# A fused retention, gated and convolution layer stack: the last product in seven products instead of eight

## The chip, the cores and the metric

One core of a Trainium2 chip. TensorE (PE) multiplies, VectorE (DVE) and ScalarE (ACT) do the elementwise work, GpSimd (POOL) here mostly issues transfers, SyncE (SP) issues transfers only. The metric is the device time in microseconds of one execution; the median over runs is what counts. A profiled execution gives a trace of every instruction, from which all rows below are read.

## The reference

Three layers on 8 batches of 576 tokens with 512 features:

```python
# 1: retention, 8 heads of 64
ret = (q @ k.T / 8 * Dmat) @ v                 # Dmat: gamma_h ** (t - s) for s <= t
x = heads of ret side by side                  # 576 x 512
# 2: gated layer with mixing over the sequence
h = gelu(x @ w_in);  u, v = h[:, :512], h[:, 512:]
v_s = w_sg @ (layernorm(v) * g_ln) + b_sg[:, None]
x = x + (u * v_s) @ w_out
# 3: convolution gate
gate = sigmoid(sum over k < 5 of conv_w[k] * x shifted down by 4 - k)
out = (gate * (x @ w_val)) @ w_out2
```

The weights w_in, w_out, w_val, conv_w and w_out2 come as 64-bit numbers. All products need more precision than one pass of the fast matmul type gives, so each operand is held as a high and a low part (a cast on ACT, then a subtraction on DVE) and each product is three matmuls: high by high, high by low, low by high.

## The kernel before, in words

**First part (to about 394 us).** Batch by batch: retention, `x @ w_in`, the mix with `w_sg`, the gate. Places for all of it are written out by hand in `plan`, `PLACES`, `KEYS`. Beside it the weights of the later layers are fetched by SP (`fetch_second`, lines 282 and 283), decoded on ACT and DVE (`decode_second`) and stored in DRAM, two of twelve row blocks per batch (`jobs`). The four blocks of w_out are also added into the seven weight operands of a Strassen product (`sums_second`, with `SUM_AT` for the places) and stored in `w7d`; w_val and w_out2 go to `wvd` as they are. The gated activations go to DRAM (`g1d`), where POOL's accumulating transfers add up the operands t1 to t4 of the same seven products (`sum_up`).

**Second part (from about 394 us).** All operations are entered with `add(engine, us, function, reads, writes, ...)`, and `Planner.order` lays them out beforehand: each engine takes the ready operation with the longest tail, PE's order is the order of entry, and transfers land by a model of one pipe. The resulting list is fixed; on the chip every engine goes through its own in order, waiting by semaphores. With `i` the batch:
- `back(i)`: the seven products of w_out (`strassen`; 12 matmuls of 128x288 each, line 1152) from operands loaded into `raw_g` and split by `split_seven`; the sums of outputs need three snapshots of PSUM by ACT (`snap`) and three DVE additions (line 1193); the residual comes by three accumulating transfers of POOL from `x1d` (line 1204).
- `conv(i)`: for each of 4 feature blocks one ACT product (line 1226), four DVE multiply-adds (line 1232) and one sigmoid on ACT.
- `value(i)`: `plain`, four blocks of 24 matmuls (line 1252), each multiplied by the gate on DVE into `f` (line 1269).
- `final(i)`: the same `plain` with w_out2 on `f`, each output copied by ACT (line 1291) and stored.

The loop enters, for each i, back(i), conv(i), final(i-2), value(i-1); the last two rounds are final(6), value(7) and then final(7). Split operands (casts of line 158, subtractions of line 161) rotate through `NPAIR` buffers. PSUM has four buffers of two banks, taken in turn. `LATE` says in which round the operand sums of the last three batches are entered.

Of the kernel before, what the change touches and what calls it, by code (L numbers as in the profile page):

```python
# [18 lines left out]
DM = H * D  # L19
# [31 lines left out]
NPAIR, NSNAP, NOUT = 5, 3, 3  # L51
AHEAD = (B - 1, 4)
LATE = {2: (B - 3, 4), 3: (B - 2, 0), 4: (B - 1, 0)}
# [80 lines left out]
def fused_kernel(  # L134
# [31 lines left out]
    wvd = dram.tile([128, 2, 2, KT, DM], F32, name="wvd")  # L166
    w7d = dram.tile([128, 7, 2, 2, 256], F32, name="w7d")
# [17 lines left out]
    with ExitStack() as p1:  # L185
# [99 lines left out]
        def decode_second(j):  # L285
            raw = raws.pop(j)
            t = raw.rearrange("p n t -> p (n t)").rearrange("p (t n) -> p t n", t=2).bitcast(F32)
            layer, k = divmod(j, KT)
            if layer:
                return decode(t[:, 0].bitcast(F32R), t[:, 1].bitcast(F32R), raw, *small_tmp(DM)) + [  # L290
                    lambda: sync.dma_start(out=wvd[:, layer - 1, :, k], in_=t)
                ]
# [7 lines left out]
        def sums_second(k):  # L300
            x, y = pairs_of.pop(k), pairs_of.pop(k + 2)
            f, g, r = (z.bitcast(F32) for z in small_tmp(DM))
            left, right = slice(0, 256), slice(256, 512)

            def put(n, src):
                sync.dma_start(out=w7d[:, n, :, k], in_=src)
# [623 lines left out]
        def plan(kind, *args):  # L930
# [29 lines left out]
            elif kind == "v":  # L960
                now += 2.79
                at(start, v_tile, *args)
                if args[1] == 3 and i in (3, 4):
                    for j in jobs(i):
                        at(start, fetch_second, j)
# [18 lines left out]
            else:  # L984
# [15 lines left out]
        def decode_at(b, place):  # L1000
# [6 lines left out]
            for n, j in enumerate(jobs(b)):  # L1007
# [42 lines left out]
        for k in range(5):  # L1050
# [15 lines left out]
            w=[q_r.tile([128, 2, KT, DM], F32R, name="wv0")],  # L1066
# [24 lines left out]
        def split_seven(raw, key, stage=1):  # L1091

            got = {}
            for p in range(4):
                names = ORDER[2 * p : 2 * p + 2]
                src = raw[:, 2 * p : 2 * p + len(names)].rearrange("p a k n -> p (a k) n")
                k, y = split(lambda src=src: src, [(key, n) for n in names], 2 * len(names), stage)
# [13 lines left out]
        add("POOL", 0.05, lambda: pool.dma_start(out=wo, in_=w7d), (), ("wo",), 2.0, 1, 3670)  # L1111
# [13 lines left out]
        count = dict(ps=0, s=0, o=0)  # L1125
# [94 lines left out]
        def conv(i):  # L1220
            for m in range(KT):
# [7 lines left out]
                for j in range(1, TAPS):  # L1229
# [8 lines left out]
        def plain(layer, xs, put):  # L1238

            def block(o, h):  # L1240
# [3 lines left out]
                def go():  # L1244
                    ps, w = got(key), L["w"][layer]
                    for mm in range(2):
                        j = 0
                        m = slice((2 * o + mm) * 128, (2 * o + mm) * 128 + 128)
                        for k in range(KT):
                            wh, wl = w[:, 0, k, m], w[:, 1, k, m]  # L1250
# [6 lines left out]
                add("PE", 3.2, go, (("hi", at), ("lo", at), ("w", layer)), (key,), 0.24)  # L1257
                put(o, h, key)

            for h in (1, 0):  # L1260
                for o in range(2):
                    block(o, h)

        def value(i):

            def put(o, h, ps):
                add(
                    "DVE", dve_us(2 * HN),
                    lambda: dve.tensor_tensor(
                        L["f"][:, 2 * h + o], full(ps), half(L["gate"][i % 2], o, h), op=ALU.mult  # L1270
                    ), (ps, *(("gate", i % 2, 2 * o + z) for z in range(2))), (("f", o, h),),
                )

            plain(0, split_x(i), put)

        def final(i):

            def put(o, h, ps):
                to = out[:, 2 * o : 2 * o + 2, i * S + h * HN : i * S + (h + 1) * HN]
                if (o, h) == (1, 0) and i == B - 1:  # L1280
# [13 lines left out]
            xs = {  # L1294
                h: split(
                    lambda h=h: L["f"][:, 2 * h : 2 * h + 2].rearrange("p a k n -> p (a k) n"),
                    [("f", o, h) for o in range(2)], stage=2,
                ) for h in (1, 0)
            }
            plain(1, xs, put)  # L1300
# [21 lines left out]
        def load_w(n):  # L1322
            add(
                "POOL", 1.0, lambda: pool.dma_start(out=L["w"][n], in_=wvd[:, n]), (("f", 0, 1),) if n else (),
                (("w", n),), 2.0, 2 if n else 1, 2100,
            )
# [4 lines left out]
        for i in range(B + 2):  # L1331
# [22 lines left out]
    L["f"] = q_o.tile([128, 4, 2, HN], F32, name="f")  # L1354
    L["w"].append(q_o.tile([128, 2, KT, DM], F32R, name="wv1"))
    L["x2"].append(q_o.tile([128, KT, PAD + S], F32, name="x2_1"))
    L["gate"] = [q_o.tile([128, KT, S], F32, name=f"gate{n}") for n in range(2)]
    L["o"] = [q_o.tile([128, 2, HN], F32, name=f"o{n}") for n in range(NOUT)]
# [99 lines left out]
```

## Time and profile before

| | |
|---|---|
| median of 3 runs | 726.21 us (725.86 to 726.44) |
| profiled execution | 727.7 us, its span from first to last instruction 725.9 us |
| mean granted clock | 0.985 of full speed; 1.00 from 50 us on |
| busy: PE, DVE, ACT, POOL | 702.0, 521.7, 358.7, 120.8 us |
| matmuls | 8754 |

PE is the matmul row, PEld the weight loads beside it. Busy times of overlapping instructions are counted once, so a group's mean times its count can exceed its busy time. A wait is put down to the one that ended it last. Batches of the second part begin at 463.0, 499.8, 536.6, 573.4, 610.2 and 646.9 us (each with its product stretch of 84 matmuls).

### The profile page before, as it was taken

To read this page: it belongs to the slowest core of one execution; us is meant where nothing else is said; L and a number is where in the kernel's file an instruction comes from. 1 tells how busy PE (TensorE), PEld (TensorE's weight loads), DVE (VectorE), ACT (ScalarE), POOL (GpSimd) and SP (SyncE) were. 2 spreads that over 40 slices of the span, in tenths; PEclk is the share of its full clock that TensorE was granted. 3 is DMA by queue.
4 is the path that set the end of the run, shared out by engine and by line. 5 is a ranking of instruction groups with operands and counts; after the bars stand their busy time and mean duration, and the time that the engine had idled before them with its cause. 6 is when DMAs were issued, how large, how long until landed. Compare 5 with 4: busy or idle time off the path is not lost.

```text
span 725.9 us, 20052 instructions
## 1 busy us (share of the span) xinstructions
PE 702.0 (97%) x8754; PEld 672.6 (93%) x8754; DVE 521.7 (72%) x830; ACT 358.7 (49%) x651; POOL 120.8 (17%) x189
## 2 busy tenths in 40 slices
PE   3789999999999999999999999999999999999997
PEld 3689889899998998998989999999999999999997
DVE  5777788796797865957747559899795959593921
ACT  5566583653753635526436047664645444534421
POOL 0000340410501204203113022020302120202000
PEclk7799999999999999999999999999999999999999
DMA  8978439689499994696835998973847774606011
GB/s 337 326 285 288 159 107 330 196 290 345 101 266 377 257 322 163 173 372 185 219 130 116 385 309 217 282 147 115 148 164 132 212 134 160 115 18 115 34 50 65
DMA packets 63830, 147.78 MB, mean 204 GB/s; under 512 B 5376, under 2 KB 39808, under 8 KB 61952
## 3 DMA queue, kind: packets, MB, share of 16 engines
q1 hardware_dynamic: 32720, 96.33, 37.1%
q0 software_dynamic: 18992, 31.46, 22.7%
q10 hardware_dynamic: 12032, 18.73, 7.1%
q8 instruction: 68, 1.11, 0.6%
q14 instruction: 18, 0.15, 0.1%
HBM read 107.97 MB, written 52.69 MB: 221 GB/s over the span
## 4 chain that ended last, share of the span: by engine, by line
PE 89%; DMA 5%; issue 2%; DVE 2%; ACT 1%; SPq 1%; ACTq 0%
PE ps L1252 28%; PE ps_u L179 14%; PE ps_v L564 14%; PE ps_m L651 11%; PE ps L1152 11%; DMA raw_g<-g1d 4%; PE sc L420 3%; PE xo L498 3%; PE xo L490 2%; PE st L436 2%; PE ps_m L659 2%; DMA qk_sb<-in_qk 1%; DVE op L161 1%; ACT op L158 0%; SPq L375 0%
## 5 line engine op out<-in xcount | busy, mean ns | idle before, releaser
L1252 PE MATMUL ps<-op,wv 128*128 128x288 f32 x1536 | 205.1, 295 | 0.0
L1252 PEld LDWEIGHTS ps<-op,wv 128*128 128x128 f32 x1536 | 204.3, 188 | 0.0
L651 PE MATMUL ps_m<-ws,vh 128*128 128x288 f32 x768 | 113.7, 297 | 0.4 <-DVE gt L668 0.4
L1232 DVE SCALAR_TENSOR_TENSOR gate<-x,cw_sb,gate 128x576 f32<-128x576 f32 x128 | 97.2, 812 | 19.4 <-ACT gate L1226 19.4
L651 PEld LDWEIGHTS ps_m<-ws,vh 128*128 128x128 f32 x768 | 104.9, 188 | 1.5 <-DVE gt L668 0.6
L1152 PE MATMUL ps<-op,wo 128*128 128x288 f32 x672 | 91.7, 297 | 0.4 <-DVE op L161 0.4
L179 PE MATMUL ps_u<-xh,wi 128*128 128x288 f32 x448 | 91.7, 297 | 0.0
L1152 PEld LDWEIGHTS ps<-op,wo 128*128 128x128 f32 x672 | 90.6, 189 | 0.6 <-DVE op L161 0.6
L179 PEld LDWEIGHTS ps_u<-xh,wi 128*128 128x128 f32 x448 | 72.6, 188 | 0.6
L564 PE MATMUL ps_v<-wi,xh 128*128 128x512 f32 x224 | 70.8, 397 | 0.0
L179 PE MATMUL ps_u<-xl,wi 128*128 128x288 f32 x224 | 66.1, 295 | 0.0
L1204 POOL DMA_DIRECT2D x<-x1d x24 | 31.4, 1565 | 167.1 <-DVE x L1193 166.8
L510 ACT COPY xg<-xo 128x768 f32<-128x768 f32 x24 | 19.1, 797 | 73.1 <-PE xo L498 66.4
L161 DVE TENSOR_TENSOR op<-raw_g,op 128x1152 fp32r<-128x1152 f32 (+1 forms) x32 | 38.0, 1204 | 22.5 <-ACT op L158 22.5
L564 PEld LDWEIGHTS ps_v<-wi,xh 128*128 128x128 f32 x224 | 41.6, 188 | 9.6 <-ACT xh L158 0.2
L668 DVE SCALAR_TENSOR_TENSOR gt<-ps_m,g_sb,b_sb 128x288 f32<-128x288 f32 x64 | 32.8, 515 | 24.2 <-PE ps_m L659 24.1
L158 ACT CAST op<-raw_g 128x1152 fp32r<-128x1152 f32 (+1 forms) x32 | 32.6, 1036 | 35.2 <-DMA raw_g<-g1d 20.7
L581 ACT ACTIVATE vt<-ps_v 128x512 f32<-128x512 f32 x36 | 21.5, 597 | 55.6 <-PE ps_v L564 55.0
L591 POOL TENSOR_SCALAR rs<-mv 128x1 f32<-128x1 f32 x36 | 10.1, 280 | 228.3 <-DVE mv L590 216.7
L400 ACT ACTIVATE kk_sb<-kk_sb,kf_sb 128x64 f32<-128x64 f32 x184 | 47.0, 336 | 2.0 <-DMA kk_sb<-in_kk 2.0
L564 PE MATMUL ps_v<-wi,xl 128*128 128x512 f32 x112 | 44.4, 396 | 0.2 <-DVE xl L161 0.2
L637 ACT ACTIVATE u<-ps_u 128x288 f32<-128x288 f32 x64 | 26.2, 409 | 35.6 <-PE ps_u L179 35.1
(112 smaller groups left out, 1107.3 us busy)
## 6 DMA issues: line engine op xcount, KB each, us to landing
qk_sb<-in_qk SPq DMA_DIRECT2D x24, 960.0 KB, 8.3
raw_g<-g1d SPq DMA_DIRECT2D x8, 2016.0 KB, 8.5
vv_sb<-in_vv SPq DMA_DIRECT2D x24, 576.0 KB, 5.7
g1d<-g1d POOLq DMA_DIRECT2D x48, 288.0 KB, 5.0
g1d<-u SPq DMA_DIRECT2D x40, 288.0 KB, 7.7
kk_sb<-in_kk SPq DMA_DIRECT2D x24, 384.0 KB, 6.3
x1d<-xg ACTq DMA_DIRECT2D x24, 384.0 KB, 6.2
x<-x1d POOLq DMA_DIRECT2D x24, 384.0 KB, 6.5
```

Of the source, the lines that this page charges most:

```text
L158: return act.copy(dst, src) if engine is act else engine.tensor_copy(dst, src)
L161: return dve.tensor_tensor(dst, src, high.bitcast(F32), op=ALU.subtract)
L179: pe.matmul(ps[:, :n], lhs, rhs[:, k, x_cols], start=i == 0, stop=i == last)
L400: act.mul(k[:, j, n], k[:, j, n], kf_sb[:, j, n : n + 1])
L564: pe.matmul(ps, lhs, rhs, start=i == 0, stop=i == KT * 3 - 1)
L637: act.activation(bt[b]["u"][:, m, t0 : t0 + w], mx.pop((b, n))[:, :w], AF.Gelu_apprx_tanh)
L651: pe.matmul(ps[:, :n], lhs, rhs, start=first, stop=False)
L668: dve.scalar_tensor_tensor(gt, mx.pop((b, i))[:, :n], g_sb[:, m : m + 1], b_sb[:, t0 : t0 + n], op0=ALU.mult, op1=ALU.add)
L1152: pe.matmul(got(ps)[:, o, :HN], lhs, rhs, start=first and i == 0, stop=last and i == 5, skip_group_check=True,)
L1204: lambda g=g, at=at: pool.dma_start(out=L["x2"][par][:, :, at : at + GT], in_=x1d[:, i * NG + g], accum_op=ALU.add), mine, [("x2", par, "g ...
L1232: lambda gt=gt, x2=x2, m=m, j=j: dve.scalar_tensor_tensor(gt(), x2(j), cw_sb[:, m, j : j + 1], gt(), op0=ALU.mult, op1=ALU.add), (*x2_keys ...
L1252: pe.matmul(ps[:, mm, :HN], lhs, rhs, start=j == 0, stop=j == 3 * KT - 1, skip_group_check=True)
```

## The change

The last layer is computed with seven products, as the second is. Its weight operands are summed beside the decoding in the first part and loaded as `wf` (3584 KB, waiting for output (0,0) of back(1); before, 2048 KB that waited for a block of value(0)). Its activation operands t1 to t4 are DVE sums in `value`, signs by the multiplication. Of its outputs (0,0) and (0,1) are DVE additions, (1,1) is an ACT copy and an accumulating transfer (but a DVE addition in the last batch), (1,0) an ACT copy. In feature blocks 2 and 3 of the convolution (batches 1 to 7) one tap is an ACT product into a buffer and an accumulating transfer. `NPAIR` is 4 instead of 5, `NOUT` 4 instead of 3. The entry order at the end is value(7), final(6), final(7), with f of the last batch in `raw_g`. `LATE` is one round earlier.

```diff
-NPAIR, NSNAP, NOUT = 5, 3, 3
+NPAIR, NSNAP, NOUT = 4, 3, 4
+BY_DMA = ((1,1),)
+NTAP = 1
+TAP_M = (2,3,)
+WF_AT = (("x2", 1, 0, 0),)
-LATE = {2: (B - 3, 4), 3: (B - 2, 0), 4: (B - 1, 0)}
+LATE = {1: (B - 3, 4), 2: (B - 2, 0), 3: (B - 1, 0)}
...
-            if layer:
+            if layer == 1:
...
-            return decode(high.bitcast(F32R), low.bitcast(F32R), raw, *small_tmp(DM)) + sums_second(k - 2)
+            return decode(high.bitcast(F32R), low.bitcast(F32R), raw, *small_tmp(DM)) + sums_second(layer // 2, k - 2)
...
-                if args[1] == 3 and i in (3, 4):
+                if args[1] == 3 and i in (3, 4, 5, 6):
...
-                if args[1] == 4 and i + 2 in (2, *range(5, B)):
+                if args[1] == 4 and i + 2 in (2, 7):
...
-            return (b - 2, b) if b < 4 else range(2 * b - 4, 2 * b - 2)
+            return ((0, 2), (1, 3), (8, 10), (9, 11), (4, 5), (6, 7))[b - 2]
...
-                if b < 4:
+                if b < 6:
...
-                for j in range(1, TAPS):
+                first = 1
+                if m in TAP_M and i:
+                    first = 2
+                    tmp = take("tap", NTAP)
+                    add(
+                        "ACT", act_us(S, True), lambda tmp=tmp, x2=x2, m=m: act.mul(got(tmp), x2(1), cw_sb[:, m, 1:2]),
+                        (*x2_keys(i), "pad"), (tmp,),
+                    )
+                    add(
+                        "POOL", 1.0, lambda gt=gt, tmp=tmp: pool.dma_start(out=gt(), in_=got(tmp), accum_op=ALU.add),
+                        (tmp, key), (key,), 2.0, kb=590,
+                    )
+                for j in range(first, TAPS):
...
+                def mul():
+                    gt = half(L["gate"][i % 2], o, h)
+                    if o == h:
+                        dve.tensor_tensor(fs(i, n), full(key), gt, op=ALU.mult)
+                    else:
+                        dve.scalar_tensor_tensor(fs(i, n), full(key), -1.0, gt, op0=ALU.mult, op1=ALU.mult)
...
+            block("t1", 0, 1)
+            block("b22", 1, 1)
+            plus("t3", "t1", "b22")
+            block("b11", 0, 0)
+            plus("t2", "t3", "b11")
+            plus("t1", "t1", "b11")
+            block("b21", 1, 0)
+            plus("t4", "t2", "b21")
...
-                add("ACT", act_us(2 * HN), lambda: act.copy(got(key), full(ps)), (ps,), (key,))
+                if s is not None and ((o, h) not in BY_DMA or i == B - 1):
+                    add(
+                        "DVE", dve_us(2 * HN), lambda: dve.tensor_tensor(got(key), full(ps), got(s), op=ALU.add),
+                        (ps, s), (key,),
+                    )
+                else:
+                    add("ACT", act_us(2 * HN), lambda: act.copy(got(key), full(ps)), (ps,), (key,))
+                if s is not None and (o, h) in BY_DMA and i < B - 1:
+                    add(
+                        "POOL", 1.0,
+                        lambda: pool.dma_start(
+                            out=got(key).rearrange("p k n -> p (k n)"), in_=got(s).rearrange("p k n -> p (k n)"),
+                            accum_op=ALU.add,
+                        ), (key, s), (key,), 2.0, kb=590,
+                    )
...
-            plain(1, xs, put)
+            strassen(lambda: L["wf"], ["wf"], split_seven(lambda: raw_g if i == B - 1 else L["f"], "g" if i == B - 1 else "f", 2), put)
...
-        for i in range(B + 2):
+        for i in range(B + 1):
...
-            if i >= 2:
+            if 2 <= i < B:
                 final(i - 2)
-            if 1 <= i <= B:
+            if 1 <= i < B:
                 value(i - 1)
+            if i == B:
+                value(B - 1)
+                final(B - 2)
+                final(B - 1)
```

## Rows read from the trace of the kernel before

**Rows 1.** The page, first part: engine, busy us, share of the span, instructions.

```profile
PE 702.0 (97%) x8754; PEld 672.6 (93%) x8754; DVE 521.7 (72%) x830; ACT 358.7 (49%) x651; POOL 120.8 (17%) x189
```

**Rows 2.** Waits of PE: line, who was waited for, us in total, times, longest us.

```profile
PE ps L1152 <- DVE op L161: 0.4, 1, 0.4
PE ps_m L651 <- DVE gt L668: 0.4, 1, 0.4
```

**Rows 3.** The chain of waits, from 463 us on: start us, us, engine, tile, line, instructions.

```profile
463.02 11.29 PE ps L1152 x84
474.31 25.50 PE ps L1252 x192
...
658.24 63.80 PE ps L1252 x480
```

**Rows 4.** Stretch, us; busy us of PE, PEld, DVE, ACT, POOL; PEclk, DMA share, GB/s.

```profile
299.00:347.00 48.00, 47.76 (x797) 44.00 (x796) 33.91 (x66) 22.60 (x51) 9.25 (x18) 1.00 0.80 260
439.00:463.00 24.00, 24.00 (x183) 24.00 (x183) 23.95 (x33) 16.68 (x22) 4.56 (x5) 1.00 0.94 255
463.00:499.80 36.80, 36.80 (x279) 36.80 (x278) 32.92 (x41) 18.98 (x25) 4.51 (x4) 1.00 0.60 166
499.80:536.60 36.80, 36.80 (x279) 36.80 (x278) 29.84 (x36) 19.45 (x25) 7.02 (x7) 1.00 0.67 165
573.40:610.20 36.80, 36.80 (x278) 36.80 (x278) 26.17 (x30) 17.71 (x23) 6.24 (x6) 1.00 0.71 183
...
684.00:722.00 38.00, 38.00 (x287) 37.79 (x285) 11.83 (x14) 10.47 (x14) 0.00 (x0) 1.00 0.16 55
```

**Rows 5.** Groups by line and shape, DVE: busy us, mean ns; idle before, us.

```profile
L1232 DVE SCALAR_TENSOR_TENSOR gate<-x,cw_sb,gate 128x576 f32<-128x576 f32 x128 | 97.2, 812 | 19.4 <-ACT gate L1226 19.4
...
L1269 DVE TENSOR_TENSOR f<-ps,gate 128x576 f32<-128x576 f32 x32 | 24.1, 756 | 20.7 <-PE ps L1252 20.3
...
L161 DVE TENSOR_TENSOR op<-f,op 128x1152 fp32r<-128x1152 f32 x16 | 21.7, 1356 | 3.8 <-ACT op L158 3.7
```

**Rows 6.** The same view, ACT.

```profile
L1226 ACT ACTIVATE gate<-x,cw_sb 128x576 f32<-128x576 f32 x32 | 23.2, 772 | 3.7 <-DMA x<-x1d 3.6
...
L158 ACT CAST op<-f 128x1152 fp32r<-128x1152 f32 x16 | 18.5, 1157 | 37.4 <-PE ps L1252 20.8 <-DVE f L1269 16.6
...
L1162 ACT COPY s<-ps 128x576 f32<-128x576 f32 x24 | 15.3, 637 | 10.7 <-PE ps L1152 10.2 <-ACT op L158 0.6
```

**Rows 7.** DVE in order of time, two stretches: start us, us; idle before in brackets.

```profile
514.77 1.54 DVE L1232 SCALAR_TENSOR_TENSOR gate<-x,cw_sb,gate 128x576 f32<-128x576 f32 x2
...
527.11 0.76 DVE L1269 TENSOR_TENSOR f<-ps,gate 128x576 f32<-128x576 f32 x1
...
584.28 1.36 DVE L161 TENSOR_TENSOR op<-x,op 128x1152 fp32r<-128x1152 f32 x1
...
592.83 1.36 DVE L161 TENSOR_TENSOR op<-raw_g,op 128x1152 fp32r<-128x1152 f32 x1 [5.04 <-ACT op L158]
596.29 3.01 DVE L1232 SCALAR_TENSOR_TENSOR gate<-x,cw_sb,gate 128x576 f32<-128x576 f32 x4 [2.10 <-ACT gate L1226]
...
611.60 1.35 DVE L161 TENSOR_TENSOR op<-f,op 128x1152 fp32r<-128x1152 f32 x1
```

**Rows 8.** POOL in order of time, the batch from 573 us on.

```profile
584.54 3.96 POOL L1204 DMA_DIRECT2D x<-x1d  x3 [12.30 <-DVE x L1193]
...
597.13 0.58 POOL L712 DMA_DIRECT2D g1d<-g1d  x1 [7.74 <-DMA g1d<-g1d]
```

**Rows 9.** DMA issues after 380 us: times, KB each, median us to landing.

```profile
x<-x1d POOLq DMA_DIRECT2D x24, 384.0 KB, 6.5
...
g1d<-g1d POOLq DMA_DIRECT2D x18, 288.0 KB, 5.7
...
wo<-w7d POOLq DMA_DIRECT2D x1, 3584.0 KB, 13.5
```

**Rows 10.** Line 318: duration ns min/median/max, first and last start us.

```profile
L318 DVE TENSOR_TENSOR da<-raw x2: 683/684/684, 154.8 to 206.9; 128x512 f32<-128x512 f32 x2
```

More of the change, by code (lines that the diff above doesn't have):

```diff
@@ L165, in fused_kernel @@
     g1d = dram.tile([128, B, 7, 2 * HN], F32, name="g1d")
-    wvd = dram.tile([128, 2, 2, KT, DM], F32, name="wvd")
-    w7d = dram.tile([128, 7, 2, 2, 256], F32, name="w7d")
+    wvd = dram.tile([128, 2, KT, DM], F32, name="wvd")
+    w7d = dram.tile([128, 2, 7, 2, 2, 256], F32, name="w7d")
     wbig = ctx.enter_context(tc.tile_pool(name="wbig", bufs=1))
@@ L288, in decode_second @@
             layer, k = divmod(j, KT)
-            if layer:
+            if layer == 1:
                 return decode(t[:, 0].bitcast(F32R), t[:, 1].bitcast(F32R), raw, *small_tmp(DM)) + [
-                    lambda: sync.dma_start(out=wvd[:, layer - 1, :, k], in_=t)
+                    lambda: sync.dma_start(out=wvd[:, :, k], in_=t)
                 ]
@@ L297, in decode_second, with sums_second @@
                 return decode(high.bitcast(F32R), low.bitcast(F32R), raw, *small_tmp(DM))
-            return decode(high.bitcast(F32R), low.bitcast(F32R), raw, *small_tmp(DM)) + sums_second(k - 2)
-        def sums_second(k):
+            return decode(high.bitcast(F32R), low.bitcast(F32R), raw, *small_tmp(DM)) + sums_second(layer // 2, k - 2)
+        def sums_second(layer, k):
             x, y = pairs_of.pop(k), pairs_of.pop(k + 2)
@@ L305, in put @@
             def put(n, src):
-                sync.dma_start(out=w7d[:, n, :, k], in_=src)
+                sync.dma_start(out=w7d[:, layer, n, :, k], in_=src)
             def high(dst, src):
@@ L1095, in split_seven @@
                 names = ORDER[2 * p : 2 * p + 2]
-                src = raw[:, 2 * p : 2 * p + len(names)].rearrange("p a k n -> p (a k) n")
-                k, y = split(lambda src=src: src, [(key, n) for n in names], 2 * len(names), stage)
+                src = lambda p=p, names=names: (raw() if callable(raw) else raw)[
+                    :, 2 * p : 2 * p + len(names)
+                ].rearrange("p a k n -> p (a k) n")
+                k, y = split(src, [(key, n) for n in names], 2 * len(names), stage)
                 for x, n in enumerate(names):
@@ L1110, in fused_kernel @@
         wo_keys = ["wo"]
-        add("POOL", 0.05, lambda: pool.dma_start(out=wo, in_=w7d), (), ("wo",), 2.0, 1, 3670)
+        add("POOL", 0.05, lambda: pool.dma_start(out=wo, in_=w7d[:, 0]), (), ("wo",), 2.0, 1, 3670)
         load_back(0)
@@ L1124, in fused_kernel @@
         PAD = TAPS - 1
-        count = dict(ps=0, s=0, o=0)
+        count = dict(ps=0, s=0, o=0, tap=0)
         def take(what, of):
@@ L1236, in conv, with fs, f_keys, value @@
                 add("ACT", act_us(S), lambda gt=gt: act.activation(gt(), gt(), AF.Sigmoid), (key,), (key,))
-        def plain(layer, xs, put):
-            def block(o, h):
+        def fs(i, n):
+            return (raw_g if i == B - 1 else L["f"])[:, ORDER.index(n)]
+        def f_keys(i, *names):
+            return [("g" if i == B - 1 else "f", n) for n in names]
+        def value(i):
+            xs = split_x(i)
+            def block(n, o, h):
                 key = take("ps", 4)
@@ L1244, in go @@
                 def go():
-                    ps, w = got(key), L["w"][layer]
+                    ps, wv = got(key), L["wv"]
                     for mm in range(2):
@@ L1255, in go, with plus, put @@
                                 j += 1
[L1257 to L1266, printed above, removed]
-                add(
[L1268 to L1271, printed above, removed]
-                )
-            plain(0, split_x(i), put)
+                add("PE", 3.2, go, (("hi", at), ("lo", at), "wv"), (key,), 0.24)
+                def mul():
[4 more added lines that the diff above has]
+                        dve.scalar_tensor_tensor(fs(i, n), full(key), -1.0, gt, op0=ALU.mult, op1=ALU.mult)
+                add("DVE", dve_us(2 * HN), mul, (key, *(("gate", i % 2, 2 * o + z) for z in range(2))), f_keys(i, n))
+            def plus(to, x, y):
+                add(
+                    "DVE", dve_us(2 * HN), lambda: dve.tensor_tensor(fs(i, to), fs(i, x), fs(i, y), op=ALU.add),
+                    f_keys(i, x, y), f_keys(i, to),
+                )
+            block("t1", 0, 1)
[6 more added lines that the diff above has]
+            plus("t4", "t2", "b21")
         def final(i):
-            def put(o, h, ps):
+            def put(o, h, ps, s):
                 to = out[:, 2 * o : 2 * o + 2, i * S + h * HN : i * S + (h + 1) * HN]
-                if (o, h) == (1, 0) and i == B - 1:
+                if s is None and i == B - 1:
                     for m, eng, queue, copy in ((0, "ACT", act, act.copy), (1, "DVE", sync, dve.tensor_copy)):
@@ L1322, in load_w @@
         def load_w(n):
[L1323 to L1326, printed above, removed]
+            if n:
+                add("POOL", 1.0, lambda: pool.dma_start(out=L["wf"], in_=w7d[:, 1]), WF_AT, ("wf",), 2.0, kb=3670)
+            else:
+                add("POOL", 1.0, lambda: pool.dma_start(out=L["wv"], in_=wvd), (), ("wv",), 2.0, 1, 2100)
         load_w(0)
@@ L1353, in fused_kernel @@
     ps_3 = ctx.enter_context(tc.tile_pool(name="ps_3", bufs=1, space=PSUM, reuse_waits="tile"))
-    L["f"] = q_o.tile([128, 4, 2, HN], F32, name="f")
-    L["w"].append(q_o.tile([128, 2, KT, DM], F32R, name="wv1"))
+    L["f"] = q_o.tile([128, 7, 2, HN], F32, name="f")
+    L["wf"] = q_o.tile([128, 7, 2, 2, 256], F32R, name="wf")
     L["x2"].append(q_o.tile([128, KT, PAD + S], F32, name="x2_1"))
     L["gate"] = [q_o.tile([128, KT, S], F32, name=f"gate{n}") for n in range(2)]
+    L["tap"] = [q_o.tile([128, S], F32, name=f"tap{n}") for n in range(NTAP)]
     L["o"] = [q_o.tile([128, 2, HN], F32, name=f"o{n}") for n in range(NOUT)]
```

10 lines of the change are left out of this document (2 added, 8 removed).

## The prediction

> **What bounds the kernel now.** I read the page's shares first: the matrix engine is busy 702.0 of 725.9 us [rows 1]. A high share can hide waits, so the waits of that engine come second: in the whole last part (everything after 394 us) it waited twice, 0.4 us for a split on DVE and 0.4 us for a gate on DVE [rows 2]. Third, the chain of waits, which there is one unbroken line of matmuls: per batch a stretch of 84 (the seven products of the second layer, 11.29 us) and one of 192 (two plain layers, 25.50 us), and at the end 480 in 63.80 us up to 722.0 [rows 3]. Fourth, the busy times by stretch: PE fills every stretch at the full clock, while DVE is full just after the turn (23.95 of 24.00 us), has 32.92 and 29.84 of 36.80 in the next two batches, and 26.17 in a settled one; ACT stands at 17.7 to 19.5 [rows 4]. So the end is set by the number of matmuls, and DVE is the engine that could take over.
>
> **What the change removes.** The last layer goes from 96 matmuls a batch (half of 25.50, 12.75 us) to seven products of 12, which by the second layer's own stretch cost 11.29 us [rows 3]. 12.75 - 11.29 = 1.46 us a batch, 8 batches: 11.7 us of the path.
>
> **What it adds on DVE, per batch.** Operations 576 wide with two tensor inputs take 0.75 us, splits 1152 wide 1.355 [rows 5].
> - Four operand sums (t3, t2, t1, t4): 4 x 0.755 = 3.0.
> - Splitting seven operands for four: three splits of 1152 and one of 576 (4.8) for two of 1152 (2.7): +2.1.
> - Two output sums, (0,0) and (0,1): +1.5. (1,1) goes to an accumulating transfer, except in the last batch (+0.75 there).
> - Two taps fewer for batches 1 to 7: 97.2 us / 128 = 0.76 each [rows 5], -1.5.
>
> Together +5.1; +6.6 for batch 0. A settled batch goes from 26.2 of 36.8 us [rows 4] to 31.3 of 35.3, 89%. That still fits, and it is why I keep PE as the bound. The cover is thinner, so I follow the turn in a ledger. Up to the end of value(1), 439 to 499.8, DVE did 23.95 + 32.92 = 56.9 us in 60.8 [rows 4]. Added there: value(0)'s sums 3.0, half of value(1)'s 1.5, final(0)'s splits 2.1 and sums 1.5, less conv(1)'s taps 1.5: +6.6, so 63.5 us for 59.3. The excess of 4.2 can fall on conv(2): its last taps ended at 516.3 and their first user began at 527.11 [rows 7], 10.8 us of slack. Value's four products each have a PSUM buffer of their own, so PE runs on for up to three more blocks (9.6 us) while a multiplication is late. From the third batch on, 35.3 - 31.3 gives back 4.0 us per batch. By amounts nothing reaches PE; by order something may, since each engine's list is fixed beforehand. What DVE queues behind a tap that waits for its transfer is splits and multiplications.
>
> **On ACT, per batch:** casts 3.5 x 1.157 for 2 x 1.157: +1.7; three snapshots at 0.637: +1.9; two output copies fewer, of the snapshots' size: -1.3; two tap products at 0.77: +1.5 [rows 6]. +3.8, 17.7 to 21.5 of 35.3 us [rows 4], covered by PE. Two of the snapshots and the copy for (1,1) must each be finished within one product (11.29 / 7 = 1.61 us); the second layer has the same pattern eight times and PE waited for none of them [rows 2]. Bounds: 0, or one cast of 1.16 us in the way of each of three, 3.5 us a batch; nearest row 0, which I take.
>
> **Four pair buffers for five.** A pair is two products, 3.2 us of PE (a block pair of the value layer 6.4). With four, a buffer freed by PE is needed again three pairs later, 9.6 us, and needs a cast and a split, 1.16 + 1.36 [rows 5, 6]. 7 us are left for queueing; cost 0, and at the other end the 5.04 us that DVE once waited for such a cast [rows 7], once a batch.
>
> **Accumulating transfers.** Three more per batch on POOL's queue. The trace has none within SBUF. Nearest: DRAM to SBUF, 384 KB, 6.5 us to landing, and DRAM to DRAM, 288 KB, 5.7 [rows 9]; I take 6. With one buffer for the tap product, ACT's second product waits for the first transfer; behind it in ACT's list stand casts and snapshots. Two in a row are 12 us. A settled batch's taps begin at 596.29 and their user comes at about 527.11 + 3 x 36.8 = 637.5 [rows 4, 7]: 41 us, of which DVE's own work for the conv needs 16 x 0.76 = 12. DMA is busy 0.71 of that stretch, sums included [rows 4]: room. Bounds 0 and the third rival.
>
> The Trainium skill (DMA: Bandwidth & Descriptors, Anatomy of one DMA) gives such a transfer 2.0 us plus its bytes at 436 GB/s. That would be 2.7 us by an estimate for 295 KB, against the 5.7 and 6.5 measured here; the traces decide, and by the page the third rival would cost 3 x (7.74 + 2.7 - 9.6) = 2.5 us and end faster.
>
> **The larger weight load.** wf is as large as wo, 3584 KB in 13.5 us [rows 9], where 2048 KB went before. It waits for output (0,0) of back(1), which comes after four of its seven products: back(1) begins at 463.02 - 12.75 - 11.29 = 439.0, so about 446.5 [rows 3]. It stands ahead of that batch's three residual transfers on POOL's queue and shares the DMA engines with them, so it lands at 460 to 466 and makes them up to 6 us later. Its user, final(0), starts at 463.02 + 11.29 = 474.3. What the residuals hold up is conv(1) and its split; DVE has no time for conv(1) before 463 anyway [rows 4]. Cost 0 to 3, taken as 0.
>
> **First part.** Two more weight pairs get nine DVE instructions each, at most 0.684 us: 6.2 a pair, in stretches like 299 to 347, where DVE has 33.91 of 48 and PE idles 0.24 [rows 4, 10]. The same work stood at 154.8 and 206.9 [rows 10], and PE's waits have no row for it. The later fetch for batches 5 and 6 has the lead that 3 and 4 already had. The sums moved one batch earlier (LATE) put up to six transfers a batch into the busier 440 to 560. Cost 0, at most 2.
>
> **The end.** value(7) now comes before final(6), so conv(7) has one layer (about 12 us) less, some 24 us after its back product instead of 36; and final(6), 11.3 us, covers the chain from value(7)'s sums to final(7)'s splits. In the last 38 us DVE is busy 11.83 [rows 4]: cost 0, at most 2. The last transfer out stays.
>
> **Sum.** The profiled execution took 727.7 us, 1.8 around its span of 725.9; the median of the runs is 726.2, 1.5 below. 727.7 - 11.7 = 716.0. For order I add 2.3 us, three times the 0.8 that PE waited in this part [rows 2], because DVE goes from 71% to 89%. 718.3, on the runs' scale 716.8.
>
> **Rivals.**
> 1. The turn is not absorbed: the 6.6 us of DVE work added there come out at PE once. For: DVE has no idle time from 439 to 463 [rows 4]. Against: PE waited for none of that. 714.5 + 6.6 = 721.1. Chance 0.16.
> 2. DVE becomes the bound, and the end comes later than before. DVE idles 10.6 us in a settled batch, of which 5.04 wait for one cast and 2.10 for one tap [rows 4, 7]. If such waits stay, a batch is 31.3 plus what stays; it decides at 36.8 - 31.3 = 5.5 us. With 7 left: 38.3 for 36.8, +1.5 in seven batches, 736.7. For: fewer buffers, more hand-overs. Against: conv work that runs over fills such holes, as from 439 to 463, where DVE idles 0.05. Chance 0.10.
> 3. Taps stand behind the sums on POOL. A sum there waited 7.74 us for the one before [rows 8]; with 6.5 to land, 14.2 us, less the 9.6 that four pairs cover: 4.6 to 5.1 us per event if ACT's list stands with it. Once in each of three batches with sums: 714.5 + 15 = 729.5. For: taps and sums share the queue in exactly these batches. Against: the list places them by assumed landings of 6.3 us (1.0 + 1.3 + 590 / 380 + 2.46 in the planner), close to the 5.7 and 6.5 of the rows. Chance 0.04.
> 4. DVE and POOL hold one another up: DVE's work becomes almost all two-input operations, and POOL issues three more transfers of 3.96 / 3 = 1.3 us [rows 8]. If each cost DVE its length, 31.3 + 3.9 = 35.2 plus the least idle that a batch had (36.80 - 32.92 = 3.9) is 39.1, +2.3 in seven batches: 742. Against: the 1152-wide split at 584.28 lay beside POOL's issues from 584.54 on and took 1.36, the one at 611.60 lay beside none and took 1.35 [rows 7, 8]. Chance 0.02. The Trainium skill states the rule (SBUF — State Buffer, Who interferes with whom): a DVE instruction with two SBUF inputs contends with a GpSimd instruction that reads SBUF; by these rows an issue is not held up.
> 5. Parts of 1 and 3 eat just the gain: 726. Chance 0.04.
>
> **How the numbers follow.** The forecast has 0.64, its own range 714.0 (no wait at all, and the 0.8 gone) to 719.5. Rival 1 adds 0.16 up to 723, so 714 to 723 leaves out the slower cases and a thin rest: 0.8. A measurement here can tell about 0.2%, 1.5 us. Faster: 0.64 + 0.16 = 0.80; within: 0.04; slower: 0.10 + 0.04 + 0.02 = 0.16.
>
> **What would show it.** Right: 768 matmuls fewer at the plain layer's line and 672 more at the product line; a batch's chain about 24.0 us for its 180 matmuls after back; PE's waits after 394 us together 2 to 4 us, scattered; DVE about 31 of 35 us in a settled batch. Wrong: a wait of PE for DVE or ACT of over 1 us in every batch (rival 2), waits for the tap's transfer on ACT in batches 5 to 7 of the sums (rival 3), one block of waits near 465 to 500 (rival 1), splits longer than 1.36 us beside POOL's issues (rival 4). A gain above 12.5 us would break the count of matmuls itself.

## The result and the profile after

717.13 us median (716.75 to 718.44), 726.33 before (725.86 to 727.14): ratio 0.9875, 95% interval 0.9858 to 0.9893. The profiled execution took 717.2 us, its span 715.4 for 725.9.

The page's first part, after [rows 1]: PE has 96 matmuls fewer and is as full as before; DVE has 46 us more.

```profile
PE 692.2 (97%) x8658; PEld 661.4 (92%) x8658; DVE 567.8 (79%) x899; ACT 387.2 (54%) x692; POOL 137.1 (19%) x210
```

PE's waits after, by line, in us, times and the longest [rows 2]. The first is at back(0), the second at two gates in the first part. The second is new; before, the only wait for a gate was at 437 us.

```profile
PE ps L1158 <- DVE op L165: 1.0, 1, 1.0
PE ps_m L655 <- DVE gt L672: 0.7, 2, 0.4
```

The chain of waits after, from back(1) on [rows 3]. A settled batch is 22.49 for its two product stretches and 12.70 for the value layer, 35.19 us for 36.79. At 446.89 the chain leaves PE for a cast, a split and an output sum, and comes back at 450.16: PE itself was busy in between, but the last product of back(1) began 0.4 us late (11.57 us from 440.46 to 452.03, where the same 84 matmuls take 11.20 in e10 below). The same happens once more, at 611.97, in back(6) (the expectations below say batch 5). The list of waits has no row for either.

```profile
440.46 6.41 PE ps L1158 x48
446.89 1.17 ACT op L162
448.08 1.36 DVE op L165
449.44 0.68 DVE x L1199
450.16 1.87 PE ps L1158 x12
452.03 12.70 PE ps L1277 x96
464.73 22.49 PE ps L1158 x168
...
663.59 25.39 PE ps L1277 x192
688.98 22.41 PE ps L1158 x168
```

Busy times after, settled batches, columns as in [rows 4]: PE full, DVE 31.5 to 32.7 of 35.2 us, ACT 21.2 to 22.7.

```profile
499.90:535.10 35.20, 35.20 (x267) 35.20 (x266) 31.49 (x38) 21.22 (x28) 7.97 (x8) 1.00 0.73 169
535.10:570.30 35.20, 35.20 (x267) 35.20 (x266) 32.66 (x40) 22.11 (x30) 11.10 (x12) 1.00 0.92 203
570.30:605.50 35.20, 35.20 (x266) 35.20 (x266) 31.98 (x38) 22.71 (x30) 9.69 (x10) 1.00 0.79 178
```

Where the time went shows best in three stretches of PE's list, which every kernel below goes through: the mix, from the second group of mix products after 250 us (257.77 before) to the value product that follows the next batch's mix (319.63; the expectations name it by batches); the turn, from there to back(1) (438.96); and the last part, from back(1) to PE's end. These rows are the ends of the mix stretch, start first: the kernel before, then the changed one, then the changed one without the weight sums (e2).

```profile
257.77 1.85 PE L651 MATMUL ps_m<-ws,vh 128*128 128x288 f32 x12
...
319.63 0.64 PE L564 MATMUL ps_v<-wi,xh 128*128 128x512 f32 x2
```

```profile
257.35 1.84 PE L655 MATMUL ps_m<-ws,vh 128*128 128x288 f32 x12
...
320.86 0.64 PE L568 MATMUL ps_v<-wi,xh 128*128 128x512 f32 x2
```

```profile
255.93 1.85 PE L659 MATMUL ps_m<-ws,vh 128*128 128x288 f32 x12
...
317.79 0.64 PE L572 MATMUL ps_v<-wi,xh 128*128 128x512 f32 x2
```

All kernels, by the same reading (us; the median with its spread, the ratio to the kernel before on the same chip). Medians and spreads leave out one slow run each of e3 (2346 us), e5 (1123), e6 (1126) and e12 (734).

| kernel | mix | last part | median (range) | ratio, 95% interval |
|---|---|---|---|---|
| before | 61.86 | 283.07 | 726.33 (725.86 to 727.14) | |
| changed | 63.51 | 271.07 | 717.13 (716.75 to 718.44) | 0.9875 (0.9858 to 0.9893) |
| changed again, c0 | 63.62 | 270.99 | 720.94 (716.07 to 725.40) | 0.9909 (0.9874 to 0.9944) |
| e1 fewer matmuls only | 61.88 | 270.32 | 713.39 (711.96 to 714.43) | 0.9815 (0.9794 to 0.9836) |
| e2 no weight sums | 61.86 | 271.08 | 716.15 (715.08 to 719.04) | 0.9856 (0.9832 to 0.9881) |
| e5 two taps left out | 63.86 | 271.48 | 723.22 (718.97 to 727.65) | 0.9944 (0.9917 to 0.9970) |
| e3 taps on DVE | 64.08 | 272.54 | 720.36 (717.91 to 725.35) | 0.9916 (0.9883 to 0.9949) |
| e4 no transfers | 63.79 | 276.24 | 722.67 (719.66 to 725.51) | 0.9944 (0.9920 to 0.9967) |
| e8 sums later | 65.98 | 271.08 | 718.84 (717.32 to 721.33) | 0.9888 (0.9866 to 0.9910) |
| e9 sums in two groups | 62.67 | 272.82 | 717.49 (716.29 to 720.89) | 0.9865 (0.9836 to 0.9893) |
| e10 five pair buffers | 63.41 | 283.55 | 725.48 (723.20 to 730.52) | 0.9982 (0.9959 to 1.0006) |
| e12 e9 and e10 | 62.41 | 278.48 | 725.50 (721.92 to 727.65) | 0.9977 (0.9957 to 0.9997) |
| e6 old end | | | 725.83 (722.07 to 732.79) | 0.9995 (0.9968 to 1.0021) |
| e6b old end, again | 64.54 | 278.35 | 723.74 (721.77 to 726.92) | 0.9954 (0.9930 to 0.9978) |

On the chips of the experiments single runs of one kernel spread over 2 to 11 us (the kernel before from 724.6 to 731.3), while the last part of four kernels with one and the same list there (changed, c0, e2, e8) agrees within 0.1 us. It does not always: e9 has that list too and took 1.7 us more, and e10 and e12 share a list and differ by 5.1. The mix lies between 63.41 and 64.54 in the seven kernels that have the changed kernel's list there (changed, c0, e5, e3, e4, e10, e6b). What else varies stands ahead of the last part: the first 75 us, and the turn (back(0) came 2.0 us late in c0 because `raw_g` took 20.26 us to land, 17.95 in the changed kernel's profile). So verdicts on an edit go by its stretch; but each stretch is read from one trace, and a difference in it counts here only where the waits that make it are shown.

Behind some waits PE also runs slower for a while. In the traces of c0, e3, e4, e6b, e8, e10 and e12 the granted clock falls to 0.50 (1.2 of 2.4 GHz) behind a wait of PE, once in each and twice in e10; in e4, for example, from 692.2 to 695.6 us. Matmuls of 288 columns then begin 0.24 us apart instead of 0.133, so those 3.4 us cost about 1.5 (an estimate from these numbers). From 50 us on, up to PE's end, the kernel before, the changed one, e1, e2, e5 and e9 have no such stretch, and not every wait is followed by one: behind e9's of 1.48 us the clock stays at 1.00.

### The profile page after: what moved, and what is told of

It reads as the page before. It is cut to its first block, busy times and chain, and to the rows that moved or that the text cites. A ratio compares the mean times of both kernels' runs of the same rounds, so it can differ in the third digit from the quotient of the medians.

```text
span 715.4 us, 20119 instructions
## 1 busy us (share of the span) xinstructions
PE 692.2 (97%) x8658; PEld 661.4 (92%) x8658; DVE 567.8 (79%) x899; ACT 387.2 (54%) x692; POOL 137.1 (19%) x210
## 4 chain that ended last, share of the span: by engine, by line
PE 87%; DVE 5%; DMA 5%; ACT 1%; issue 1%; SPq 1%; DVEq 0%; ACTq 0%
PE ps L1158 24%; PE ps_u L183 14%; PE ps L1277 14%; PE ps_v L568 14%; PE ps_m L655 10%; PE sc L424 3%; DMA raw_g<-g1d 3%; PE xo L502 2%; PE xo L494 2%; DMA qk_sb<-in_qk 2%; PE st L440 2%; PE ps_m L663 2%; DVE op L165 1%; DVE xl L165 1%; ACT op L162 0%
## 5 line engine op out<-in xcount | busy, mean ns | idle before, releaser
L1277 PE MATMUL ps<-op,wv 128*128 128x288 f32 x768 | 102.7, 294 | 0.0
L1277 PEld LDWEIGHTS ps<-op,wv 128*128 128x128 f32 x768 | 101.9, 188 | 0.0
L1158 PE MATMUL ps<-op,wf 128*128 128x288 f32 x672 | 90.8, 296 | 0.0
L1158 PEld LDWEIGHTS ps<-op,wf 128*128 128x128 f32 x672 | 90.1, 188 | 0.0
L1250 DVE SCALAR_TENSOR_TENSOR gate<-x,cw_sb,gate 128x576 f32<-128x576 f32 x114 | 87.5, 812 | 1.0 <-ACT gate L1232 1.0
L162 ACT CAST op<-raw_g 128x1152 fp32r<-128x1152 f32 (+1 forms) x36 | 36.7, 1036 | 46.1 <-PE ps L1277 20.5
L1168 ACT COPY s<-ps 128x576 f32<-128x576 f32 x48 | 30.8, 641 | 37.9 <-PE ps L1158 35.5
L585 ACT ACTIVATE vt<-ps_v 128x512 f32<-128x512 f32 x36 | 21.5, 597 | 53.8 <-PE ps_v L568 53.3
L1210 POOL DMA_DIRECT2D x<-x1d x24 | 31.3, 1542 | 84.1 <-DVE x L1199 83.2
L165 DVE TENSOR_TENSOR op<-raw_g,op 128x1152 fp32r<-128x1152 f32 (+1 forms) x36 | 42.9, 1202 | 5.5 <-ACT op L162 5.5
```

Of the source, the lines that this page charges most:

```text
L162: return act.copy(dst, src) if engine is act else engine.tensor_copy(dst, src)
L165: return dve.tensor_tensor(dst, src, high.bitcast(F32), op=ALU.subtract)
L585: act.activation(vt, vs[b, s][0], AF.Gelu_apprx_tanh)
L1158: pe.matmul(got(ps)[:, o, :HN], lhs, rhs, start=first and i == 0, stop=last and i == 5, skip_group_check=True,)
L1210: lambda g=g, at=at: pool.dma_start(out=L["x2"][par][:, :, at : at + GT], in_=x1d[:, i * NG + g], accum_op=ALU.add), mine, [("x2", par, "g ...
L1250: lambda gt=gt, x2=x2, m=m, j=j: dve.scalar_tensor_tensor(gt(), x2(j), cw_sb[:, m, j : j + 1], gt(), op0=ALU.mult, op1=ALU.add), (*x2_keys ...
```

## The experiments

**c0, the changed kernel again.**

> The changed kernel again, as the control of its group. Every theory: 717.1 us (716.8 to 718), 0.9875 of the kernel before. What it tells apart is the first part: its trace lost 1.7 us against the kernel before between 250 and 328 us. Theory sums (the weight sums of w_out2 on DVE hold up the gates of the mix): the same two waits of PE for a gate, about 0.45 and 0.25 us, stand in the mix of the fifth and sixth batch again. Rival chance (an accident of that execution): they are gone or elsewhere.

The two waits for a gate stand again in the mix, 0.44 and 0.24 us, and the stretch takes 63.62 (63.51 first, 61.86 before): not an accident. The time of the whole was a miss: 720.94 us, where 716.8 to 718 was expected. On this chip the change gains 6.1 us by the medians (727.05 to 720.94), though the interval of the ratio overlaps the first one. The profile of c0 lost 3.8 us of it in the turn, 123.2 us for 119.4: 2.0 are the wait for `raw_g`, about 1.5 the half clock behind it (0.50 from 426.6 to 430.0 us).

**e1, the number of matmuls alone.** On the kernel before:

```diff
+                        n = KT - 1 if layer and mm else KT
-                        for k in range(KT):
+                        for k in range(n):
...
```

> The kernel before with 21 of the 24 matmuls in each block of the last layer (part of the last product is left out), so PE does as many matmuls as in the changed kernel, and nothing is added on any engine. Theory count (PE sets the end, and the gain is the number of matmuls alone): 726.3 - 96 x 0.1328 = 713.6 us, that is 3.5 below the changed kernel: what its additions cost. Rival order (a part of the gain comes from the new order at the end or from transfers in place of DVE work): the gain here is smaller than 10 us, 716.5 or more.

713.39 us, near the 713.6 worked out (from 726.3; the kernel before had 727.05 on this chip). The chain of e1: two layers take 23.90 us for 180 matmuls, and 444 end the kernel without a break.

```profile
459.97 11.29 PE ps L1152 x84
471.26 23.90 PE ps L1253 x180
...
647.23 59.02 PE ps L1253 x444
```

The last part falls by 12.75 us with nothing but matmuls gone. The changed kernel reaches 12.0 of these; all it adds there costs 0.75, and its two late products, 0.4 us each, account for that.

**e2, no weight sums in the first part.**

```diff
+            if layer:
+                no = lambda: None
+                return [no, no, no, lambda: [put(0, x[:, :, left]), put(1, y[:, :, left]), put(2, y[:, :, right])],
+                        no, no, no, no, no, no, both(3, x), no, no, both(5, y)]
```

> The changed kernel without the additions and splits that make the seven weight operands of w_out2 in the first part (their seven stores per pair stay, with unsummed data). Theory sums (these 18 DVE and 4 ACT instructions hold up gates of the mix): 717.1 - 1.7 = 715.4 us, and no wait of PE for a gate between 250 and 330 us. Rival fetch (the later fetch or the more numerous stores cost it) and rival chance: 717.1, the 1.7 us stay or vary.

The mix takes 61.86 us, to the hundredth that of the kernel before, with the later fetch and all 28 stores in place. So the sums, with the casts and splits of their results, cost the 1.65 us, not the fetch or the stores. The trace of the changed kernel shows how: DVE at 258 us, start and length, and PE behind it. Three steps of the weight sums (lines 326, 329, 332) stand between the attention's work (452, 474, 165) and the gate (672), which ends at 261.69; PE then stands 0.45 us. The bracket counts idle time only. By the starts of the groups of matmuls, compared with the kernel before, the groups behind three gates (261.75, 308.18 and 312.22 us) slip by 0.60, 0.40 and 0.23 us, and four other places by 0.1 each: together 1.65.

```profile
257.40 0.95 DVE L452 TENSOR_TENSOR pt<-sc,dm_sb 128x768 f32<-128x768 f32 x1
258.27 0.87 DVE L474 TENSOR_TENSOR sums<-st,sums 128x256 f32<-128x256 f32 x2
259.06 0.41 DVE L326 SCALAR_TENSOR_TENSOR dt<-da,ds 128x256 f32<-128x256 f32 x1
259.51 0.42 DVE L329 SCALAR_TENSOR_TENSOR dt<-dt,da 128x256 f32<-128x256 f32 x1
259.97 0.43 DVE L332 TENSOR_TENSOR da<-da 128x256 f32<-128x256 f32 x1
260.31 0.95 DVE L165 TENSOR_TENSOR xl<-xg,xh 128x768 fp32r<-128x768 f32 x1
261.18 0.51 DVE L672 SCALAR_TENSOR_TENSOR gt<-ps_m,g_sb,b_sb 128x288 f32<-128x288 f32 x1
```

```profile
261.75 1.87 PE L655 MATMUL ps_m<-ws,vh 128*128 128x288 f32 x12 [0.45 <-DVE gt L672]
```

**e5, a lighter DVE.**

```diff
-                for j in range(first, TAPS):
+                for j in range(first, 3):
```

> The changed kernel without taps 3 and 4 of the convolution: eight DVE instructions of 0.76 us fewer per batch, DVE at about 26 of 35 us in a settled batch, the rest as it is. Theory count (PE sets the end, DVE's 90% are covered): at most the two waits of the last part go, 717.1 - 0.8 = 716.3 us. Rival DVE (the fuller DVE holds PE up in many small places that the list of waits does not show): 2 us or more come back, 715 or less.

DVE falls from 32.66 to 26.03 us in the batch that begins with back(4), and nothing comes back: the last part takes 271.48. The late products are still there, now in back(1), back(2) and back(7). So DVE's load was covered, and these waits belong to the order of the list, not to its fullness. Its median of 723.2 us, where 716.3 was expected, has no trace: the profiled execution was the fastest, 719.0, with back(1) 1.6 us later than in the changed kernel's profile and 0.4 us more behind it. Why its other runs took longer stays open.

```profile
537.10:572.30 35.20, 35.20 (x266) 35.20 (x266) 26.03 (x30) 22.78 (x30) 9.21 (x10) 1.00 0.85 194
```

**e3, no tap by transfer:** `TAP_M = ()`.

> The changed kernel with all taps on DVE again (no tap by transfer): 14 DVE instructions of 0.76 us more in the last part, DVE at 32.7 to 34.2 of 35.2 us in a settled batch. The last part is read from the start of back(1) to PE's end (before 283.1 us, changed 271.1). Theory count (DVE's work is covered as long as it fits a batch): 271.1 to 271.8 there, 717 us in all. Rival DVE (DVE is the bound in waiting; the taps had to go): each tap comes out, +1.5 us a batch, 281 there and no gain over the kernel before.

272.54, 0.7 over the upper end of what was expected, and 720.36 us in all for 717 (its turn lost 3.6 us, as c0's did). The late last product of back, 0.4 us, now comes in six batches, 1 and 3 to 7; four more of them than in the changed kernel make the 1.5 us. The chain of e3 shows one of them, with the same cast, split and sum as above:

```profile
503.56 6.47 PE ps L1158 x48
510.10 1.17 ACT op L162
511.29 1.36 DVE op L165
512.64 0.68 DVE x L1199
513.37 13.06 PE ps L1158 x96
```

**e4, neither taps nor an output sum by transfer:** `TAP_M = ()`, `BY_DMA = ()`.

> The changed kernel without both kinds of accumulating transfer: taps on DVE, and the output sum (1,1) on DVE too. DVE at 33.5 to 34.9 of 35.2 us in a settled batch, and the sum (1,1) must free its PSUM buffer within one product of 1.6 us. Theory count: it still fits by amount; with under 1 us a batch left the order begins to cost, 272 to 276 us in the last part (changed 271.1). Rival DVE: 2.3 us a batch come out, 287. A third view (DVE's load does not matter at all up to 100%): 271.1.

276.24, just over the upper end of what was expected, and in another place: only back(1) has a late product, the batches before the end run at 35.19 us, and the cost is at the end. Final(6) waits for a multiplication of value(7), which stands behind the last conv on DVE; it begins 4.0 us late. Behind this hole the granted clock is 0.51 from 692.2 to 695.6 us, about 1.5 us more. PE in e4, and the row of the stretch behind the hole (columns as in [rows 4]):

```profile
691.84 13.39 PE L1158 MATMUL ps<-op,wf 128*128 128x288 f32 x87 [3.81 <-DVE raw_g L1289]
```

```profile
692.20:695.60 3.40, 3.40 (x17) 3.40 (x16) 3.40 (x5) 1.79 (x2) 0.00 (x0) 0.51 0.02 5
```

**e6, the old order at the end.**

```diff
+                final(B - 2)
                 value(B - 1)
-                final(B - 2)
                 final(B - 1)
```

> The changed kernel with the entry order of before at the end: final(6), value(7), final(7). Theory count: final(7)'s first pair needs, after the third block of value(7), a multiplication, two sums, a cast and a split (0.75 x 3 + 1.16 + 1.36 and five hand-overs of about 0.2: 5.8 us), of which the fourth block covers 3.2: PE waits 2.6 us once, the last part is 273.7 us (changed 271.1). Rival order (the new order is worth nothing, other work covers it): 271.1.

Its runs had a median of 725.83 us, no faster than the kernel before (0.9995) and slower than either account. Where the time goes was read from a second profile:

> The changed kernel with the old entry order at the end once more, for a profile at the full clock (its first profile ran at 0.556 throughout). Its runs were some 5 us slower than the changed kernel, where 2.6 had been worked out for one place. Corrected theory: final(6) too follows its value product directly in this order, so there are two such places of 2.6 us, and the last part is 271.1 + 5.2 = 276.3 us, with PE waiting at the start of final(6) and of final(7). Rival (another engine or a transfer at the end): the waits stand elsewhere.

278.35 us, 7.3 above the changed kernel. PE waits where the corrected theory put it, for the cast and the split of the first pairs of final(6) and final(7):

```profile
680.26 0.40 PE L1158 MATMUL ps<-op,wf 128*128 128x288 f32 x1 [0.79 <-ACT op L162]
...
681.68 8.59 PE L1158 MATMUL ps<-op,wf 128*128 128x288 f32 x62 [1.02 <-DVE op L165]
...
706.44 0.40 PE L1158 MATMUL ps<-op,wf 128*128 128x288 f32 x1 [0.65 <-ACT op L162]
...
707.91 12.31 PE L1158 MATMUL ps<-op,wf 128*128 128x288 f32 x79 [1.07 <-DVE op L165]
```

From the start of back(7) (643.86 here, 641.10 in the changed kernel) to PE's end it takes 76.9 us for 70.3: 6.6, of which the late product of back, now in back(7) too, is 0.4. The two places cost 2.2 and 2.1 us before the second matmuls of final(6) and final(7), near the 2.6 worked out for each. What the theory lacked is the clock: final(7) goes slower than final(6) by the chain of e6b, and behind its hole the granted clock is 0.54 in the mean for 3.5 us, where final(6) has 1.00 throughout (columns as in [rows 4]):

```profile
681.68 11.41 PE ps L1158 x83
...
707.91 12.86 PE ps L1158 x83
```

```profile
681.60:692.90 11.30, 11.22 (x83) 11.22 (x84) 10.97 (x14) 6.63 (x9) 0.86 (x1) 1.00 0.07 12
707.90:711.40 3.50, 3.49 (x15) 3.49 (x16) 2.56 (x3) 1.31 (x2) 0.00 (x0) 0.54 0.00 0
```

The old order at the end would have taken more than half of the 12.0 us that the last part gained.

**e8, the weight sums 8 us later.**

```diff
+        SUM_LATER = (9.0, 10.0, 11.5, 11.7, 13.3, 13.4, 13.5, 14.9, 15.2, 16.4, 16.8, 17.0, 18.0, 19.2)
...
-                    for x in SUM_AT:
+                    for x in SUM_AT if b < 4 else SUM_LATER:
```

> The changed kernel with the sums of w_out2's operands in the first part started 8 us later after the decoding (the last steps at about the old places), where DVE's list has gaps. Theory sums (the sums held up two gates of the mix by falling right behind a burst of attention work): the stretch from the second mix product of the fifth batch to the value product of the seventh, 61.9 us before and 63.5 changed, falls to 61.9 to 62.3, and the whole to 715.5 us. Rival amount (it is DVE's added time in the stretch, wherever it stands): 63.5 stays, 717.1.

A miss: 65.98. No mix product waits for a gate any more, as the theory said. But the edit also closed the gap between the first stores and the cast that overwrites what they read. ACT stood 10.06 us for the store, and the value product behind it waited 2.31; then the granted clock was 0.56 from 278.6 to 282.0, and the two make the 4.1 us over the kernel before (ACT, PE, and the row of the stretch behind the wait in e8):

```profile
272.57 0.62 ACT L162 CAST raw<-dt 128x512 fp32r<-128x512 f32 x1 [10.06 <-DMA w7d<-raw]
```

```profile
278.32 0.73 PE L568 MATMUL ps_v<-wi,xh 128*128 128x512 f32 x2 [2.31 <-DVE gt L672]
```

```profile
278.60:282.00 3.40, 3.40 (x10) 2.65 (x10) 1.28 (x4) 0.00 (x0) 1.07 (x3) 0.56 1.05 375
```

**e9, the weight sums in two groups,** with the stores and the casts in their old places.

```diff
-            return [
+            steps = [
...
+            return steps[1:4] + steps[:1] + steps[4:] if layer else steps
...
+        SUM_SPLIT = (2.1, 3.6, 3.8, 9.0, 9.8, 10.8, 11.8, 12.6, 14.0, 15.2, 16.4, 16.6, 17.6, 19.0)
...
-                    for x in SUM_AT:
+                    for x in SUM_AT if b < 4 else SUM_SPLIT:
```

> The changed kernel with the sums of w_out2's operands (first part) in two groups: what the first stores need (one sum and the sign) stays in its place, the other five go some 8 us later into gaps of DVE's list, and the casts that wait for the stores stay where they were. Theory sums (the sums held up gates of the mix because they fell behind a burst; in the run with all of them later, ACT stood 10.1 us for a store and that made the loss): the stretch from the second mix group of the fifth batch to the value product of the seventh falls from 63.5 us to about 62.4 (61.9 without the sums). Rival amount (the loss goes with DVE's time there, wherever it stands): 63.5.

62.67, and 62.41 with the same edit in e12: the place decides, as the theory said, and half of the loss or more can be had back. By the whole, e9 can't be told from the changed kernel (0.9865 and 0.9875, the intervals overlap). Its last part, with the changed kernel's list, lost 1.5 us at the start of final(0), to a copy of back(2)'s output on ACT:

```profile
481.03 9.86 PE L1160 MATMUL ps<-op,wf 128*128 128x288 f32 x72 [1.48 <-ACT x L1198]
```

The copy stands on ACT behind a product of the convolution, which waited 2.27 us and began at 476.62. At 476.47 the last residual of back(1) had landed; it had been issued behind the load of `wf`. That is 34.3 us after back(1) began; in the changed kernel it is 30.5 us (470.81). e6b lost 0.6 us at the same place, at 33.1 us.

**e10, five pair buffers:** `NPAIR, NSNAP, NOUT = 5, 3, 3`, and **e12**, e9 and e10 together.

> The changed kernel with five buffers for split operands, as before the change (and three output buffers, for the room). Theory buffers (with four, the cast of an operand of value waits until the second pair of back is free, its split stands ahead of an output sum on DVE, and the last product of back waits 0.4 us for that sum, in batches 1 and 5): the last part falls from 271.1 to 270.3 us, both waits gone. Rival (three output buffers or DVE's load cost as much): 271.1 or more.

> Both of the other edits of this group, the sums in two groups and five buffers: if both theories hold, 717.1 - 1.1 - 0.8 = 715.2 us, the fastest so far; in the trace the two stretches must show both savings at once, 62.4 and 270.3 us.

The rival holds. The late products at back(1) (11.20 us in one piece) and back(6) are gone, but the last part takes 283.55, and PE now waits for the copies of outputs on ACT (line 1329) and once for a split, in e10:

```profile
440.58 11.20 PE ps L1158 x84
```

```profile
563.13 7.05 PE L1277 MATMUL ps<-op,wv 128*128 128x288 f32 x41 [2.47 <-ACT o L1329]
...
648.80 11.43 PE L1158 MATMUL ps<-op,wo 128*128 128x288 f32 x63 [3.48 <-DVE op L165]
...
714.11 6.13 PE L1158 MATMUL ps<-op,wf 128*128 128x288 f32 x44 [1.32 <-ACT o L1329]
```

The waits come to 7.8 us, and behind two of them the clock is halved, for 10.2 us in all, some 4.5 us more by the estimate above. The longest wait begins on ACT, which stood 5.06 us ahead of conv(7):

```profile
641.66 1.44 ACT L1232 ACTIVATE gate<-x,cw_sb 128x576 f32<-128x576 f32 x2 [5.06 <-issue]
```

Before that product ACT issues the store of an output, at 640.42, just after the accumulating transfer `o<-s` had landed at 640.34 (issued at 629.73). In e12, with the same list, that transfer took 7.5 us instead of 10.6, ACT stood 1.57 us there, and this hole of PE is not there. So part of e10's loss varies from run to run. The other holes are in both, and whether the third output buffer alone makes them, or the list that the planner makes with five pairs, stays open: the two were changed together, for room. e12 has the better mix (62.41) but not the 270.3 (278.48); no version of the group beats the changed kernel clearly.

## Why the prediction was right

716.8 was forecast, 717.13 measured. PE set the end, as forecast, and the gain is its matmuls less small waits; that the two numbers lie 0.3 us apart is luck. By the profiles the gain is 10.5 us where 9.4 were forecast: 1.1 too little for the matmuls and 1.5 too much for order in the last part, against 1.65 that the first part was not charged with. The medians moved by 9.2 because the profiled execution of before was 1.4 above its median and that of after 0.1.

- **What sets the end.** PE still does: e1 gives what 96 matmuls fewer are worth by themselves, and e5 shows that a lighter DVE gives nothing.
- **The removed time, 11.7 us,** was under-sized. It took the seven products at the second layer's 11.29; in the last layer they came to 22.49 - 11.29 = 11.20, and value to 12.70 for 12.75 [rows 3]. A batch fell from 36.79 to 35.19, 1.60 us for 1.46; eight times 1.60 is 12.8, and e1 says 12.75. So the sign "a gain above 12.5 us would break the count" was drawn too low: the count alone gives more.
- **DVE's ledger.** 31.3 of 35.3 us were forecast, 31.5 to 32.7 of 35.2 measured; ACT 21.5 and 21.2 to 22.7. Nothing of it reached PE by its amount, at the turn either: the last part holds 0.75 us of cost, not rival 1's 6.6.
- **The allowance for order, 2.3 us** (three times 0.8 is 2.4), was put in the last part, where it came to 0.75; 2 to 4 us of waits after 394 us were forecast, and the list has 1.0. **The first part, "cost 0, at most 2",** took 1.65 (c0, e2): that is the step with the wrong value. It argued from two earlier batches in which the same sums stood beside a PE without a wait, and from DVE's load in a stretch. Here they fall right behind attention work, and the load of the stretch (17.57 of 22.00 us, 251 to 273) does not show that.
- **Four pair buffers,** costed at 0: by the trace the buffer that comes free late makes the cast late, its split stands ahead of an output sum, and PE loses 0.4 us, twice. With five pairs (e10) both are gone, but the list is another there, and with four pairs the late products move with the list (e5, e4), so the buffers alone are not shown to be the cause.
- **The larger weight load,** costed at 0 of 0 to 3: it was issued at 451.89, not about 446.5, and landed at 466.73, not by 466, the residuals behind it by 470.81. No wait of PE came of it in the changed kernel's profile, but 1.5 us in e9's and 0.6 in e6b's.
- **The end,** costed at 0 with at most 2: right, and the other side was not priced: with the old order two places would have cost 6 us (e6b), about 1.5 of them by the clock.
- **Rival 2** had its threshold at 5.5 us of idle time in a batch. In the last part of e3 DVE is busy 250.90 of 272.6 us, and it costs 1.5; in e4 254.09 of 276.2, and it costs 5.2, most of it one hole at the end and the clock behind it. So the two kinds of transfer are worth 5.2 us together by these traces, but not because every batch would overflow.
- **Rival 3.** After 394 us ACT waited twice for a tap's transfer, 4.0 us in all, and the list of PE's waits has none behind them.
- **Rival 4.** Splits of 1152 took 1.352 to 1.354 us in the mean after, with POOL issuing more, and 1.356 before [rows 5].
- **Sum.** By the profiles: first 75 us and what follows -0.4 (it varies from run to run), mix +1.65, turn +0.1, last part -12.0, after PE's end +0.2: -10.5, the difference of the spans.

## What to carry to other kernels

When a product is traded for sums on a second engine, price the matmuls from the stretch they leave, check the second engine's free time per batch, and then look at three places separately: where the new work lands in another stage's list, where a buffer's release now stands ahead of something that PE needs soon, and where a product directly follows the one that makes its operands. The last was worth some 6 us here, half of the gain; a different layer in between covers it. A hole of PE can cost more than its length: behind several of them here the granted clock was halved for a while, about 1.5 us more each. A step put later helps only if what waits for its stores moves with it (e8 against e9).

## What the runs showed of the hardware

Accumulating transfers from SBUF to SBUF, 288 KB each, landed sooner than the two kinds before them [rows 9]. The DMA issues after 380 us of the changed kernel:

```profile
gate<-tap POOLq DMA_DIRECT2D x14, 288.0 KB, 4.8
...
o<-s POOLq DMA_DIRECT2D x7, 288.0 KB, 3.8
```

These are medians; one `o<-s` of e10 took 10.61. The prediction had taken 6 us. The Trainium skill's fit (DMA: Bandwidth & Descriptors, Anatomy of one DMA), 2.7 us by the same estimate, lies below both; with other traffic beside them (DMA busy 0.73 to 0.92 of these batches) the measured numbers decide.
